# A gated convolution and token MLP on one core: the first filter block in two parts, the last copy-out on ScalarE alone, and a new order of issue

## The chip, the core and the metric

The kernel runs on one core of a Trainium2 chip. A core has a matrix engine (TensorE, PE), a vector engine (VectorE, DVE), a scalar engine (ScalarE, ACT), a general engine (GpSimd, POOL), and a sync engine (SP) that here only issues transfers. Each engine works through its own list of instructions in order, and waits at an instruction until the semaphores it names are reached. SBUF is the on-chip memory, PSUM the small memory that PE writes. The metric is the device time of one execution in microseconds (us); lower is better.

## The reference, cut to what matters

```python
# S = 2048 positions, D = 640 channels, F = 1536, all inputs bf16; x = A_q
g  = sigmoid((x * gate_w).sum(-1, keepdims=True))
# a: a short shift convolution of k, times v, then a causal convolution of length S per channel
kv = (sum of 4 shifted copies of k, weighted by shift_k) * v
y  = irfft(rfft(pad(kv)) * rfft(pad(ssm_k)))[:S]          # "filter" ssm_k is (D, S)
a  = x * (y + kv * ssm_D)
# b: an MLP over the positions
h  = layernorm(x)
u  = gelu(einsum("sd,sf->df", h, w1) + b1)
b  = (einsum("df,fs->ds", u, w2) + b2).transpose(0, 2, 1)
out = g * a + (1 - g) * b
```

## The kernel before, in words

**The MLP.** x comes in as 16 tiles of 128 positions (`xs`). DVE takes mean and variance of a tile (two `bn_stats` at L884, one `bn_aggr` at L886), POOL turns the variance into 1/sqrt (`vpe`, then `rstd`, L666 and L659), and DVE writes the normalised tile `h` (L667). PE multiplies all 16 tiles by 12 column blocks of w1 (384 matmuls, "h,w"), ACT applies gelu and writes `gT`. The second product (384 matmuls, "gT,w") has 16 groups of 24; ACT adds the bias and multiplies by 1-g on the way out (`o`).

**The convolution.** S is cut into 4 blocks of 512. A filter block i is loaded to `wnat{i}`, folded by DVE into `en` (even and odd part, L659), turned by PE (40 small matmuls against the identity, for blocks 0 and 1; blocks 2 and 3 are turned by a transposing transfer), copied from PSUM by ACT to `eo`, multiplied by cosine and sine tables `TFc` and `TFs`, which ACT makes at the start, and copied by ACT to its spectrum `W{i}`. A block of kv goes the like way: k through the shift matmuls (`kT,dg`), ACT to `ks`, a transposing transfer to `kn`, times v on DVE, DVE sums `es` and `fs`, PE by the tables `AFs` and `AFc`, ACT to the spectrum `A{j}`. DVE then multiplies spectra, 10 pairs of blocks, into `Z` (with `tT` for the second product); PE transforms each of 4 sums back ("Z,TI", 32 matmuls each), and the two halves of a result are copied out of PSUM as `pb` and `qb`, combined by DVE to `cg`, multiplied by the gated x (`xe`, scaled on ACT), and added to the output: by accumulating transfers from POOL, except the last block's forward rows, where DVE adds `o` itself and SP stores `cg`.

**What sets the order.** Every operation is declared by helpers that record it (`pe`, `act`, `tt`, `ts`, `vop`, `dma`), with its reads and writes. Nothing is emitted then. At the end `plan.run(ORDER)` emits all operations in the order of a tuple of operation numbers, numbered as they were declared. So ORDER is the order of every engine's list, of SP's and POOL's transfers too. A tracker adds the waits. PSUM is four slots (`pp0` to `pp3`), handed out in the order of emission: an operation that opens a slot gets the one that was given back first, and waits for the last reader of that slot.

The lines that the steps below touch: `W_PARTS` (how a filter block is cut for load, fold and turn), `wnat_load`, `w_turn`, and `epilogue` for the last block (`last`), where DVE makes `pb` from PSUM (L1224) while ACT makes `qb` (L701). Transfers of filter and x are at L278, `kT` at L265, POOL's gathers at L271 and its accumulating scatters at L269 and L273.

```python
W_PARTS = [((0, 2), (2, DC)) if i == 0 else ((0, DC),) for i in range(P)]   # DC = 5 chunks of 128 channels
```

The block whose turn comes first is block 1: its load is SP's first transfer, its fold is DVE's first work on data, and its turn is PE's first work. Before, it is one load, two folds and four turns of five chunks; block 0, which follows, is already cut into chunks 0-1 and 2-4.

Of the kernel before, what the change touches and what calls it, by code (L numbers as in the profile page):

```python
# [11 lines left out]
ACT = mybir.ActivationFunctionType  # L12
# [306 lines left out]
def bass_gated_mix__ssm_conv_h3__mixer_token_mlp__prompt_kernel(  # L319
# [7 lines left out]


ORDER = (
# [32 lines left out]
)  # L362


# [123 lines left out]
def _build(nc, A_q, A_k, A_v, A_shift_k, A_ssm_k, A_ssm_D, B_x, B_w1, B_b1, B_w2, B_b2, gate_w, out):  # L488
# [4 lines left out]
    P = 4  # L493
# [5 lines left out]
    DC = D // 128  # L499
# [4 lines left out]
    with ExitStack() as es:  # L504
# [237 lines left out]
        def two(p_):  # L742
            return lambda: pp[p_.slot][:, :].rearrange("p (c f) -> p c f", c=2)[:, :, 0:HD]

        def flat(p_):
            return lambda: pp[p_.slot][:, 0:D]

        def h2(ap):
            return ap.rearrange("p (c f) -> p c f", c=2)
# [112 lines left out]
        def w1t(s_, t):  # L862
            return b[f"w1_{(2 * s_ + t // 8) % 3}"][:, t % 8, :]

        W_PARTS = [((0, 2), (2, DC)) if i == 0 else ((0, DC),) for i in range(P)]

        def wnat_load(i, pr):
            for c0, c1 in W_PARTS[i]:
# [6 lines left out]
        for gi, g in enumerate(groups):  # L875
# [4 lines left out]
            for k, t in enumerate(g):  # L880
                for c in range(2):
                    o_ = b["stats"][:, t, c * 6:(c + 1) * 6]
                    i_ = xs[:, k, c * HD:(c + 1) * HD]
                    vop("DVE", 0.41, (lambda o_, i_: lambda e: e.bn_stats(o_, i_))(o_, i_), [i_], [o_], pr)  # L884
                o_, i_ = b["mv"][:, t, :], b["stats"][:, t, :]
# [28 lines left out]
        p_ = _PS()  # L914
# [9 lines left out]
        def w_turn(i):  # L924
            wn = b[f"wnat{i}"]
            en = b[f"en{i % 2}"]
            eo = b[f"eo{i % 2}"]
            for c0, c1 in W_PARTS[i]:
                fw = wn[:, c0:c1, 256:512].rearrange("p c (k u) -> p k c u", k=2)
                bw = bass.AP(tensor=wn, offset=256 + c0 * n, ap=[[DC * n, 128], [-128, 2], [n, c1 - c0], [-1, 128]])  # L930
                for e, op in ((0, ALU.add), (1, ALU.subtract)):
                    tt(en[:, 2 * e:2 * e + 2, c0 * 128:c1 * 128].rearrange("p k (c u) -> p k c u", c=c1 - c0), fw, bw, op,
                       1.0 + 0.1 * i)
            x0 = en[:, 2, :].rearrange("p (c u) -> p c u", c=DC)[:, :, 0:1]
            if i == 0:
                tt(x0, wn[:, :, 0:1], b["bf"][:, FT + NT:FT + NT + DC].rearrange("p (c o) -> p c o", o=1), ALU.add, 1.0)
            else:
                copy(x0, wn[:, :, 0:1], 1.0 + 0.1 * i, "DVE")
            if i in WTD:
                dma(eo[:, :, :, :].rearrange("p e k (c d) -> p (e k c) d", c=DC),  # L940
                    en[:, :, :].rearrange("p k d -> p (k d)"), f"eo{i % 2}", 0.5, turn=True)
                return
            for e in range(2):
                for k in range(2):
                    p_ = _PS(True)
                    for c0, c1 in W_PARTS[i]:
                        pe([p_], [(p_, c * 128, 128, en[:, 2 * e + k, c * 128:(c + 1) * 128], ident, True, True)
                                  for c in range(c0, c1)], 1.0 + 0.1 * i)
                    act(eo[:, e, k, :], flat(p_), ACT.Copy, 0.3, ps=[p_])

        def split(dst, src, pr):
            tt(dst[:, 0:2, :], src[:, 0:2, :], src[:, 2:4, :], ALU.add, pr)
# [53 lines left out]
        for s_ in range(1, NSET):  # L1006
            w1_load(s_, 2.5 if s_ < 2 else 6.0 + 2 * s_)
            for fi in range(FSET):
                p_ = _PS(True)
# [193 lines left out]
        def epilogue(m_, res, pr):  # L1203
# [13 lines left out]
            for i in range(2):  # L1217
                P_, Q_ = res[2 * i], res[2 * i + 1]
                pb, qb = (b["pb"][:, i, :], b["qb"][:, i, :]) if m_ else (b["pb0"][:, 0, :], b["qb0"][:, 0, :])
                act(h2(qb), two(Q_), ACT.Copy, 0.4, ps=[Q_])  # L1220
                if not last:
                    act(h2(pb), two(P_), ACT.Copy, 0.4, ps=[P_])
                else:
                    vop("DVE", 0.77, (lambda o_, s_: lambda e: e.tensor_copy(o_, s_()))(h2(pb), two(P_)),  # L1224
                        [two(P_)], [pb], 0.4, ps=[P_])
                if m_ == 0 or last:
                    for k, op in ((1, ALU.subtract), (0, ALU.add)):
                        c_ = cgs[k][:, i, :]
                        tt(c_, pb, qb, op, 20)
                        if last:  # L1230
                            tt(c_, c_, xes[k][:, i, :], ALU.mult, pr)
                            if k:
                                t_ = 4 * m_ + 3 - 2 * i
                                dma(rows1(out, t_), c_, f"acc1_{i}_{m_ % 2}", 1.0, stream="POOL", accum=True, idx=back(t_), whole=whole(out))
                            else:
                                tt(c_, c_, b[f"o1_{q + i}"][:, 0, :], ALU.add, pr)
                                dma(rows1(out, 4 * m_ + 2 * i), c_, "last", 1.0)
# [47 lines left out]
        p_ = _PS()  # L1285
# [43 lines left out]
```

## Time and profile before

| | |
|---|---|
| runs shown | 191.5, 192.04, 192.24 us; median 192.04 |
| the profiled execution | 191.21 us, of which its span (first to last instruction) 189.3 |
| granted TensorE clock, mean | 0.997 |
| PE busy | 175.3 us (93%), 1636 matmuls |
| DVE busy | 176.4 us (93%), 216 instructions |
| ACT busy | 111.1 us (59%), 171 instructions |
| POOL busy | 67.6 us (36%), 84 instructions |
| moved by DMA | 38.04 MB |

The profile page lists busy time by engine, the span in 40 slices, transfers, the chain of work that ended last, and the costliest groups of instructions. The timeline lists instructions in order of time as "start, duration, engine, line, operation, out<-in, shape, count"; in brackets stands the idle time of the engine just ahead and what ended it. A row with a count above 1 is several instructions run together. The list of waits has "who <- for whom: us in total, times, longest". PEld is the loading of weights beside PE; SPq are transfers as SP issues them. Where a helper records every operation all have its line (L659 for DVE's two-input operations, L701 for ACT, L310 for PE), so tiles are named.

### The profile page before, as it was taken

What the parts mean: (1) busy time and instruction counts of PE and PEld (TensorE: products, weight loads), DVE (VectorE), ACT (ScalarE), POOL (GpSimd) and SP (SyncE); (2) the same over time, 40 slices, a digit from 0 to 9 for tenths busy, and PEclk for the clock granted to TensorE, in tenths of its full rate; (3) what the DMA queues carried; (4) which work ended last, traced back from release to release, by engine and by line L of the source; (5) the groups of instructions that cost most, each with busy time, mean ns of one, the idle gap of its engine ahead of it and who ended that gap; (6) DMA issues with size and microseconds to landing.
All of it is one profiled execution on the core that took longest, in us unless ns stands there. A gap on an engine that the chain in (4) does not pass through costs nothing.

```text
span 189.3 us, 3968 instructions
## 1 busy us (share of the span) xinstructions
PE 175.3 (93%) x1636; PEld 123.5 (65%) x1636; DVE 176.4 (93%) x216; ACT 111.1 (59%) x171; POOL 67.6 (36%) x84
## 2 busy tenths in 40 slices
PE   0699999999999998999999999999999999999780
PEld 0666677666668755777777767677777777776550
DVE  4889997984999999999999999999999999999992
ACT  5889978069997077613235278633840938551660
POOL 7216557950000004000000000090058995788481
PEclk9999999999999999999999999999999999999998
DMA  4999969799994999299883568517389798696796
GB/s 146 329 248 329 361 192 237 218 272 184 244 221 126 162 257 233 68 275 236 230 205 65 118 142 239 165 40 201 117 272 281 201 207 284 117 208 192 140 149 128
DMA packets 78078, 38.04 MB, mean 201 GB/s; under 512 B 42476, under 2 KB 77548, under 8 KB 78060
## 3 DMA queue, kind: packets, MB, share of 16 engines
q1 hardware_dynamic: 75324, 32.87, 67.6%
q0 software_dynamic: 2736, 4.92, 13.2%
q8 instruction: 13, 0.21, 0.4%
q14 instruction: 5, 0.04, 0.1%
HBM read 23.08 MB, written 4.92 MB: 148 GB/s over the span
## 4 chain that ended last, share of the span: by engine, by line
PE 57%; DVE 26%; ACT 5%; issue 4%; DMA 3%; POOL 2%; DVEq 0%; POOLq 0%; ACTq 0%
PE pp L310 57%; DVE stats L884 5%; DVE W L659 5%; DMA w<-in_B_w_dram 3%; DVE Z L659 3%; DVE h L667 3%; DVE cg L659 2%; DVE kn L659 2%; DVE tT L659 2%; DVE es L659 1%; POOL vpe L666 1%; DVE mv L886 1%; DVE fs L659 1%; DVE dg L659 1%; ACT TFs L701 1%
## 5 line engine op out<-in xcount | busy, mean ns | idle before, releaser
L310 PE MATMUL pp<-h,w 128*128 128x320 bf16 x384 | 54.7, 299 | 0.3 <-ACT grow L701 0.3
L310 PE MATMUL pp<-gT,w 128*128 128x320 bf16 x384 | 53.4, 299 | 0.1
L659 DVE TENSOR_TENSOR tT<-A,W 128x5120 bf16<-128x5120 bf16 (+2 forms) x18 | 45.4, 2524 | 3.5 <-ACT A L701 3.3
L310 PEld LDWEIGHTS pp<-h,w 128*128 128x128 bf16 x384 | 36.7, 98 | 16.2 <-issue 2.1
L310 PEld LDWEIGHTS pp<-gT,w 128*128 128x128 bf16 x384 | 37.3, 98 | 14.9 <-DMA w<-in_B_w_dram 0.4
L659 DVE TENSOR_TENSOR Z<-Z,tT 128x2560 bf16<-128x2560 bf16 (+5 forms) x29 | 46.4, 1624 | 0.2
L271 POOL DMA_INDIRECT xe<-in_A_q_dram,bidx x8 | 19.4, 2428 | 62.7 <-DVE fs L659 49.2
L701 ACT ACTIVATE A<-pp 128x640 bf16<-128x640 f32 x32 | 20.6, 708 | 10.2 <-PE pp L310 9.7
L701 ACT ACTIVATE gT<-pp,bf 128x640 bf16<-128x640 f32 x12 | 9.4, 793 | 23.9 <-PE pp L310 18.4
L701 ACT ACTIVATE o<-pp,c,omg 128x640 bf16<-128x640 f32 x16 | 13.9, 880 | 14.1 <-PE pp L310 14.0
L271 POOL DMA_INDIRECT vn<-in_A_v_dram,bidx x8 | 10.4, 1294 | 31.3 <-DVE kn L659 29.8
L310 PE MATMUL pp<-Z,TI 128*128 128x320 bf16 x128 | 18.5, 299 | 1.0 <-ACT o L701 1.0
L269 POOL DMA_INDIRECT out_dram<-cg,bidx x8 | 17.8, 2229 | 2.6 <-issue 1.8
L310 PEld LDWEIGHTS pp<-Z,TI 128*128 128x128 bf16 x128 | 12.3, 98 | 6.2 <-ACT o L701 1.3
L701 ACT ACTIVATE W<-pp 128x640 bf16<-128x640 f32 x24 | 15.4, 752 | 0.4 <-PE pp L310 0.4
L884 DVE BATCH_NORM_STATS2 stats<-xs 128x6 f32<-128x320 bf16 x32 | 13.4, 465 | 0.0
L310 PE MATMUL pp<-eo,TFc 128*128 128x320 bf16 x64 | 11.7, 300 | 0.1
L659 DVE TENSOR_TENSOR Z<-A,W 128x5120 bf16<-128x5120 bf16 x4 | 11.3, 2817 | 0.0
L310 PE MATMUL pp<-eo,TFs 128*128 128x320 bf16 x64 | 11.1, 313 | 0.0
L701 ACT ACTIVATE ks<-pp 128x1024 bf16<-128x1024 f32 (+1 forms) x12 | 10.0, 900 | 1.0 <-PE pp L310 1.0
L701 ACT ACTIVATE xe<-xe,ggr 128x640 bf16<-128x640 bf16 x8 | 6.5, 822 | 6.6 <-DMA xe<-in_A_q_dram,bidx 6.5
L310 PE MATMUL pp<-idp,en 128*128 128x128 bf16 x40 | 4.5, 290 | 6.2 <-POOL cst L677 6.2
(101 smaller groups left out, 211.0 us busy)
## 6 DMA issues: line engine op xcount, KB each, us to landing
w<-in_B_w_dram SPq DMA_DIRECT2D x8, 768.0 KB
w<-in_B_w_dram SPq DMA_DIRECT2D x10, 512.0 KB, 4.6
xs<-in_A_q_dram SPq DMA_DIRECT2D x7, 320.0 KB, 5.1
wnat<-in_A_ssm_k_dram SPq DMA_DIRECT2D x3, 640.0 KB, 4.5
out_dram<-o SPq DMA_DIRECT2D x6, 320.0 KB, 4.4
vn<-in_A_v_dram SPq DMA_DIRECT2D x4, 320.0 KB, 4.1
xe<-in_A_q_dram SPq DMA_DIRECT2D x4, 320.0 KB
w<-in_B_w_dram SPq DMA_DIRECT2D x4, 256.0 KB, 5.8
```

The lines of the kernel that those rows point to most:

```text
L269: ins = engobj.indirect_dma_start(whole, off, in_ap, None, compute_op=ALU.add)
L271: ins = engobj.indirect_dma_start(out_ap, None, whole, off)
L310: ins = self.nc.tensor.matmul(ps_ap, lhsT=lhsT, rhs=rhs, start=start, stop=stop)
L659: return vop(eng, c, lambda e: e.tensor_tensor(out_, in0, in1, op), [in0, in1], [out_], pr)
L666: return e.tensor_scalar(out_, in0, s1, None, op0=op0)
L667: return e.tensor_scalar(out_, in0, s1, s2, op0=op0, op1=op1)
L701: return e.activation(out_, src, func, **kw)
L884: vop("DVE", 0.41, (lambda o_, i_: lambda e: e.bn_stats(o_, i_))(o_, i_), [i_], [o_], pr)
L886: vop("DVE", 0.16, (lambda o_, i_: lambda e: e.bn_aggr(o_, i_))(o_, i_), [i_], [o_], pr)
```

## The change

Three edits, the third of which reaches every engine.

1. `W_PARTS` cuts block 1 as block 0 is cut. Its load becomes two transfers (256 and 384 KB), its two folds four (512 and 768 elements a row), each of its four turns two steps of 2 and 3 matmuls. The sum of the work is the same; seven operations are added (719 become 726).
2. In the last block's epilogue both `pb` copies go from DVE (`tensor_copy`) to ACT.
3. ORDER is another permutation throughout.

```diff
-        W_PARTS = [((0, 2), (2, DC)) if i == 0 else ((0, DC),) for i in range(P)]
+        W_PARTS = [((0, 2), (2, DC)), ((0, 2), (2, DC)), ((0, DC),), ((0, DC),)]
...
-                    act(eo[:, e, k, :], flat(p_), ACT.Copy, 0.3, ps=[p_])
+                    if (i, e, k) in ():
+                        vop("DVE", 0.83, (lambda o_, s_: lambda q_: q_.tensor_copy(o_, s_()))(eo[:, e, k, :], flat(p_)),
+                            [flat(p_)], [eo[:, e, k, :]], 0.3, ps=[p_])
+                    else:
+                        act(eo[:, e, k, :], flat(p_), ACT.Copy, 0.3, ps=[p_])
...
-                if not last:
-                    act(h2(pb), two(P_), ACT.Copy, 0.4, ps=[P_])
-                else:
-                    vop("DVE", 0.77, (lambda o_, s_: lambda e: e.tensor_copy(o_, s_()))(h2(pb), two(P_)),
-                        [two(P_)], [pb], 0.4, ps=[P_])
+                act(h2(pb), two(P_), ACT.Copy, 0.4, ps=[P_])
```

The condition `in ()` never holds, so that piece changes nothing. Of ORDER, its ends (the middle is left out):

```diff
-    12, 11, 13, 9, 14, 10, 21, 0, 15, 22, 24, 1, 5, 23, 17, 31, 2, 155, 16, 32, 36, 26, 27, 25, 29, 28, 203, 204, 6,
...
-    717, 697, 707, 543, 708, 718, 709,
+    12, 9, 13, 11, 14, 10, 21, 22, 155, 26, 15, 5, 0, 24, 23, 27, 1, 203, 28, 204, 16, 25, 31, 217, 32, 156, 205,
...
+    720, 713, 701, 704, 663, 712, 722, 714, 721, 550, 706, 715, 716, 723, 724, 725,
```

In words, by engine and place ("i0" and "i1" are the two 128-row halves of the last block's result; c is the cosine, s the sine side):

| place | before | after |
|---|---|---|
| SP, first issues | block 1; bias row; block 0 chunks 2-4, 0-1; three bias rows; x tiles 0, 4-5; shift weights; x 1, 2-3, 6-7; k block 0 (turning); x 8-9, 14-15 ... | block 1 chunks 0-1, 2-4; bias row; block 0 chunks 2-4, 0-1; bias row; shift weights; bias row; x tile 1; bias row; x 0, 2-3, 4-5, 6-7, 10-11, 8-9; k block 0 (turning); x 14-15 ... |
| DVE, head | table indices; fold block 1 (2); indices; fold block 0; statistics | table indices; fold block 1 chunks 0-1 (2); chunks 2-4 (2); indices; fold block 0; statistics |
| PE, head | block 1: four turns; part of block 0; first table product is block 1 by TFs | one part-turn of block 1; its other seven; part of block 0; first table product is block 1 by TFc |
| ACT, head | TFs, index, TFc, TFs, index, then four `eo` | TFs, two indices, TFc, TFc, then four `eo` |
| POOL, normalisation | `vpe`/`rstd` of tile 1 before tile 0; a gather of v after both | `vpe` of tiles 0 and 1, `rstd` of 0; a gather of v; `vpe`/`rstd` of 2-3, of 4-5; then `rstd` of tile 1 |
| DVE, before the kv block 0 sums | fold of block 3 before the last `h`; `kn`, two `es`, two `fs`, fold of block 2 | fold of block 3 among the last `h`; `kn`, `es`, fold of block 2, `es`, two `fs` |
| PE, kv block 0 | w1 group, `fs` by AFs (2), w1 group, `es` by AFs (2), then AFc | `es` by AFs (2), w1 group, `fs` by AFs (2), w1 group, then AFc |
| PE, last inverse | i0 with Z of frequency rows 1, 2, 3, 0; i1 with 1, 2, 3, 0 | i0 with 1, 2, 3; i1 with 1; i0 with 0; i1 with 2, 3, 0 |
| PE, mlp groups ahead of it (a, b: first and second of a pair) | 7b, 7a, 6b; 6a is PE's last work | 7a, 7b, 6b; 6a is PE's last work |
| DVE, last Z pieces | rows 1-3 of the real half are closed after row 0's first product and its sum | rows 1-3 of the real half are closed after row 0's first product, ahead of its sum |
| ACT, end | qb i0; xe1 i1; qb i1; xe0 i1; xe0 i0; last `o` | qb i0; pb i0; pb i1; qb i1; xe1 i1; xe0 i0; last `o`; xe0 i1 |
| DVE, end | pb i0; cg1 i0 (2); pb i1; cg1 i1 (2); cg0 i0, i1; cg0 i1 (times x, plus o); cg0 i0 (times x, plus o) | cg1 i0 (2); cg1 i1 (2); cg0 i0, i1; cg0 i0 (times x, plus o); cg0 i1 (times x, plus o) |

60 rows, old and new, of the table ORDER are left out of this document.

## The prediction

> **What bounds the kernel now.** I read the page's shares first, then the list of waits of DVE, then the timeline of the head and of the tail. From the page:
>
> ```profile
> PE 175.3 (93%) x1636; PEld 123.5 (65%) x1636; DVE 176.4 (93%) x216; ACT 111.1 (59%) x171; POOL 67.6 (36%) x84
> PE 57%; DVE 26%; ACT 5%; issue 4%; DMA 3%; POOL 2%; DVEq 0%; POOLq 0%; ACTq 0%
> ```
>
> Two engines are equally full, and the chain that ended last changes between them. All of DVE's waits, from the list of waits:
>
> ```profile
> DVE tT L659 <- ACT A L701: 3.3, 1, 3.3
> DVE ncol L674 <- POOL ncol_i L767: 1.6, 1, 1.6
> DVE en L659 <- DMA wnat<-in_A_ssm_k_dram: 1.2, 1, 1.2
> DVE h L667 <- POOL rstd L659: 1.2, 1, 1.2
> DVE en L659 <- ACT bf L701: 0.6, 1, 0.6
> ```
>
> The 3.3 is the last of them in time: it ends at 45.42, with the first product into `tT`. From there to its last sum at 185.69 DVE shows no wait. So **what DVE gains before 45.4 comes out at the end, if the tail lets it**. PE has no wait over 0.1 us between 74.5 and the last inverse either. The head, from the timeline:
>
> ```profile
> 5.29 0.84 DVE L659 TENSOR_TENSOR en<-wnat 128x1280 bf16<-128x1280 bf16 x1 [1.24 <-DMA wnat<-in_A_ssm_k_dram]
> 6.19 2.53 PE L310 MATMUL pp<-idp,en 128*128 128x128 bf16 x22 [6.19 <-POOL cst L677]
> 6.94 2.49 ACT L701 ACTIVATE eo<-pp 128x640 bf16<-128x640 f32 x4 [0.47 <-PE pp L310]
> 8.51 1.27 PE L310 MATMUL pp<-eo,TFs 128*128 128x320 bf16 x4
> 11.67 0.72 PE L310 MATMUL pp<-eo,TFs 128*128 128x320 bf16 x4
> ```
>
> PE starts 0.06 us after the first fold; the "POOL cst" named as its releaser was long done. ACT waits only 0.47 for the turns. The tail:
>
> ```profile
> 175.29 0.89 ACT L701 ACTIVATE o<-pp,c,omg 128x640 bf16<-128x640 f32 x1 [2.65 <-PE pp L310]
> 176.23 4.51 PE L310 MATMUL pp<-Z,TI 128*128 128x320 bf16 x32 [0.97 <-ACT o L701]
> 176.85 0.89 DVE L659 TENSOR_TENSOR Z<-Z,tT 128x640 bf16<-128x640 bf16 x2
> 179.25 0.82 DVE L1224 CAST pb<-pp 128x640 bf16<-128x640 f32 x1
> 180.57 3.42 PE L310 MATMUL pp<-gT,w 128*128 128x320 bf16 x24
> 181.04 0.82 DVE L1224 CAST pb<-pp 128x640 bf16<-128x640 f32 x1
> 184.03 0.88 ACT L701 ACTIVATE o<-pp,c,omg 128x640 bf16<-128x640 f32 x1
> 185.20 0.49 DVE L659 TENSOR_TENSOR cg<-cg,o 128x640 bf16<-128x640 bf16 x1
> ```
>
> Z's last piece ends at 176.85 + 0.89 = 177.74, DVE's last sum at 185.69, 7.95 later; the span ends 3.6 after that (store and closing).
>
> **The change, step by step.**
>
> *1. Block 1 in parts, DVE.* Until 5.29 DVE has nothing but indices, done at 4.06. The first 256 KB of block 1 now land alone. No row shows that landing; it lies between 3.5 (the shortest landing of an x tile, 3.5 us from issue, would give 0.73 + 3.5 = 4.2) and 5.26. I take 4.2, as that transfer (160 KB) is the nearest row. Two folds of 512 elements (0.42 each, as block 0's) then lie in the old wait: 0.85. Against it, block 0's pairs of part-folds took 0.90 and whole folds 0.84 each, so cutting costs 0.12. DVE is **0.73 ahead**; with the landing at 5.26 it would be 0.12 behind. The second load is issued some 0.5 later than the one whole load; its bytes are the same, so I let it land at 5.3.
>
> *2. ACT and PE in the head.* ACT's five table operations end at 6.47 in both orders (a constant on POOL comes two small instructions later: up to 0.3), so of its 0.47 wait 0.2 to 0.47 goes. PE's first part-turn comes at about 4.8, but it then stands for the second folds and for block 0's. Up to 10.7 its matmuls run at half speed: the 4 by TFs took 1.27 at 8.51 and 0.72 at 11.67. Counted at these rates it has done three 320-wide matmuls more and three small ones fewer by then, 0.25; with ACT's gain, 24 copies of 0.62 to 0.75 in a row, I take **0.3 for PE** (ends 0 and 0.6).
>
> *3. DVE through the statistics.* The 0.62 wait for `bf` stays nearly whole (bf's matmul now stands behind two table products; I reckon 0.5). The 1.16 wait for `rstd` goes: of POOL's pairs (0.45 + 0.74) the late one now precedes its `h` by 1.7 us, by summing POOL's rows. One 0.1 operation moves ahead. Together 0.73 + 0.1 + 1.16 - 0.1 = 1.9 earlier at the product `kn`: 33.8 in place of 35.7, 34.6 by summing the new order's rows piece by piece. `kn` itself is ready at about 30.7 (before, its last transposing transfer was issued at 27.3; they take 3.4).
>
> *4. The way to the first Z.* Fold of block 2 (1.75) now precedes the second `es`, where before it filled the 3.3 wait. From `kn` the `fs` end after 1.41 + 5 x 0.8 + 1.6 = 40.5 to 41.1; before, 40.36. So the 1.3 of step 3 is spent here, to shrink the wait; PE does the `es` products first (1.1), which were after. Then the four AFs copies need one matmul pair and ACT (0.6 + 3 x 0.7, a gelu among them): `tT` starts at 43.5 to 43.8 (45.42). The product by A's cosine side needs four more copies behind a w1 group and a gelu: 46.9 to 47.3 against 48.25 before. DVE **gains 1.3** here; I bound it by 0.7 (ACT alone 0.75 ahead) and 1.7.
>
> *5. The middle.* PE's small waits at 40.05 (0.44), 71.2 (0.53) and 73.5 to 74.5 (0.34) stood before `fs` and `es` products; the new order puts a gate product and the sine side first, so I count them gone: with 0.3, PE is up to 1.6 ahead. DVE's list is nearly the old one; comparing sums of rows, `kn` of block 1 comes after its transfers, the W sums after their copies by 0 to 1. What a wait here would cost is bounded by 0 and 3.3, the longest that DVE shows; I take 0.
>
> *6. The tail.* The 0.97 before the inverse goes: counted through ORDER, its first slots are given back by older groups. But Z bounds it: rows 1-3 close one operation (0.82) earlier, at 176.08 - 0.82 - 1.3 = 174.0, and row 0 at 177.74 - 1.3 = 176.45, one step (0.55) later needed. Thence: four steps 2.2, last mlp group 3.4, `o` 0.9, then `xe0 i1`, now behind `o`, 0.75, and two operations of DVE 1.0: 8.3 after Z. Before it was 7.95. The casts (2 x 0.82) leave DVE, but DVE then waits for `o`, so this buys nothing; ACT's two copies (0.70 each) lie in the time when it waits for the last group. The end therefore moves by **-1.3 + 0.35 = -0.95**. If the inverse could start with PE alone (173.7), Z would still hold it.
>
> *Queues moved past.* The k transfer, which holds SP from 6.89 to 12.05, is now issued after x tiles 8 to 11, about 8.0; its product is needed at 20. The w1 and w2 loads keep their places up to one.
>
> **The sum.** 191.21 (the profiled execution; 189.3 and 1.9 around) - 0.95 = 190.3; the median stands 0.83 above that execution: 192.04 - 1.0 = **191.0**.
>
> **The rivals.**
>
> *A. The gain dies on the way* (chance 0.22). Only 0.4 of DVE's lead reaches Z, because ACT's copies hold it: they run without pause from 44.1 to past 60. For it: ACT is 9/10 busy there. Against: ACT also starts earlier. Then -0.4 + 0.35: 192.0.
>
> *B. Slow clock* (0.08). The half speed lasted 4.5 us from PE's first matmul, and PE was never idle in them. If it is unbroken work that ends it, the new order's stands only from about 7.8 on, after its waits for folds, and half speed lasts to 12.3: 1.6 us of it lose 0.8, and the `fs` products and `tT` come 0.4 to 0.8 later. Then -1.3 + 0.7 + 0.35: 191.8. Against: one execution can't say what ended it. [...]
>
> *C. Slower: POOL's chain* (0.18). `rstd` of tile 1 now stands behind a gather and two pairs, and PE's second w1 step needs its `h`; tile 8's pair stands behind another gather. The slack of either is 1.7 to 1.9 by POOL's rows with gathers at 1.29 (v's mean). A gather at 2.43 (x's mean) adds 1.14, two 2.3. From 1.8 on each us is lost by DVE; at 3.6 all of 1.3 and 0.5 more: 0.35 + 0.6 slower, 193.0. For it: this wait was there before, 1.16. Against: v's gathers are the same ones.
>
> *D. More than forecast* (0.08): step 3's lead passes whole (1.9), and DVE's saved casts shorten the tail: 190.1.
>
> The forecast has 0.44, from 190.5 to 191.6. **Range** 190.1 to 193.0, the ends of C and D.
>
> 0.5% (0.96 us) is about what a measurement here can tell. The forecast lies on that bound: six tenths of it and D are faster, 0.34; A, B and the rest of the forecast the same, 0.48; C slower, 0.18.
>
> **What would show it.** Step 1: first fold before 5.0, and a row of 512 elements ahead of PE's start. 3: no `h <- rstd` wait in DVE's list. 4: `tT` before 44.2, the next `Z` before 47.4. 5: DVE without waits from there. 6: no 0.97 ahead of the inverse, Z's last piece at 176.4, the last sum 8.3 later, and DVE waiting for ACT in between. Wrong if a wait of over 0.5 stands in DVE's list after 47, or the first fold starts after 5.2.

## The result, and the profile after

The changed kernel took 190.32 us (median of 7 runs, 189.77 to 191.4), the kernel before 192.09 beside it (7 runs); the ratio is 0.9919, 95% interval 0.9895 to 0.9942. The forecast was 191.0, range 190.1 to 193.0. Measured a second time, 12 runs beside 35 of before, the changed kernel took 191.36 against 191.85: 0.9977 (0.9959 to 0.9996). Both intervals lie below 1, and they do not overlap; by how much the kernel is faster is the question of most of what follows.

The profiled execution of the changed kernel took 190.03 us, its span 188.0 (before: 191.21 and 189.3). From its page, the busy shares and the chain that ended last:

```profile
PE 175.3 (93%) x1636; PEld 124.1 (66%) x1636; DVE 175.2 (93%) x216; ACT 112.6 (60%) x173; POOL 65.1 (35%) x84
...
PE 89%; DMA 7%; DVE 1%; ACT 0%; ACTq 0%; SPq 0%; issue 0%
```

PE and DVE are as full as before. That the chain now names PE alone means only that the walk back from the end took PE's side of two parallel full engines. The list of waits says more (DVE <- whom: us in total, times, longest):

```profile
DVE tT L659 <- ACT A L701: 2.6, 1, 2.6
...
DVE cg L659 <- ACT pb L701: 1.0, 1, 1.0
DVE en L659 <- DMA wnat<-in_A_ssm_k_dram: 0.9, 2, 0.7
DVE en L659 <- ACT bf L701: 0.7, 1, 0.7
...
DVE Z L659 <- ACT A L701: 0.5, 1, 0.5
```

The wait of `h` for `rstd` (1.2 before) is gone, the one for `A` is 0.7 shorter, and a new one for the copy `pb` stands in the tail. The head, from the timelines of DVE and of PE:

```profile
3.84 0.77 DVE L659 TENSOR_TENSOR en<-wnat 128x512 bf16<-128x512 bf16 x2 [0.21 <-DMA wnat<-in_A_ssm_k_dram]
...
5.58 1.04 DVE L659 TENSOR_TENSOR en<-wnat 128x768 bf16<-128x768 bf16 x2 [0.69 <-DMA wnat<-in_A_ssm_k_dram]
...
43.76 2.83 DVE L659 TENSOR_TENSOR tT<-A,W 128x5120 bf16<-128x5120 bf16 x1 [2.63 <-ACT A L701]
47.12 2.83 DVE L659 TENSOR_TENSOR Z<-A,W 128x5120 bf16<-128x5120 bf16 x1 [0.54 <-ACT A L701]
```

```profile
4.67 0.61 PE L310 MATMUL pp<-idp,en 128*128 128x128 bf16 x4 [4.67 <-DVE par_i L666]
6.20 2.87 PE L310 MATMUL pp<-idp,en 128*128 128x128 bf16 x23 [0.93 <-DVE en L659]
```

The first part is folded 1.45 earlier than block 1 was (5.29), PE starts at 4.67 and stands again to 6.20, and `tT` starts at 43.76 in place of 45.42. The tail:

```profile
171.45 3.43 PE L310 MATMUL pp<-gT,w 128*128 128x320 bf16 x24 [1.57 <-DMA w<-in_B_w_dram]
...
174.72 4.51 PE L310 MATMUL pp<-Z,TI 128*128 128x320 bf16 x32
...
175.44 0.90 DVE L659 TENSOR_TENSOR Z<-Z,tT 128x640 bf16<-128x640 bf16 x2
...
182.22 1.55 POOL L269 DMA_INDIRECT out_dram<-cg,bidx  x1 [0.30 <-DVE cg L659]
182.53 0.89 ACT L701 ACTIVATE o<-pp,c,omg 128x640 bf16<-128x640 f32 x1 [0.53 <-PE pp L310]
...
184.69 0.49 DVE L659 TENSOR_TENSOR cg<-cg,o 128x640 bf16<-128x640 bf16 x1
```

The last piece of Z ends at 176.34 (177.74 before), DVE's last sum at 185.18 (185.69), the span at 188.0. So 1.40 of lead reach Z, 0.51 the last sum, and 1.3 the end: between last sum and end 0.8 came from somewhere that the prediction had taken as fixed. By its own signs the prediction was already in trouble here: it called itself wrong if a wait of over 0.5 stood in DVE's list after 47, and one of 0.54 stands at 47.12.

Six moments of every trace, in us from the start of its span, carry most of what follows. "bf" is the start of the small operation `en<-wnat,bf` of block 0, the one that waits for `bf`; "second tT" is the product into `tT` with kv block 1.

| kernel | bf | kn | first tT | second tT | last Z ends | span |
|---|---|---|---|---|---|---|
| before | 12.11 | 35.67 | 45.42 | 76.31 | 177.74 | 189.3 |
| changed | 12.46 | 34.85 | 43.76 | 74.98 | 176.34 | 188.0 |
| changed, again (e5) | 12.12 | 34.52 | 43.43 | 75.93 | 177.29 | 189.3 |
| e1 new head, old rest | 12.72 | 35.12 | 44.69 | 76.20 | 177.64 | 189.6 |
| e2 old head, new rest | 11.93 | 35.49 | 45.24 | 76.40 | 177.76 | 189.5 |
| e3 changed, block 1 whole | 12.14 | 34.53 | 43.44 | 75.92 | 177.28 | 189.4 |
| e9 changed, gate product late | 12.08 | 34.47 | 43.38 | 74.61 | 176.90 | 188.7 |
| e10 before, `rstd` moved | 12.52 | 36.64 | 46.39 | 77.28 | 178.72 | 190.8 |
| e11 block 1 whole, gate late | 12.37 | 34.76 | 43.68 | 74.91 | 176.38 | 188.4 |
| e12 before, block 1 in parts | 11.76 | 35.31 | 45.06 | 75.95 | 177.40 | 189.5 |

Read across, the columns keep fixed distances. In the new order the first `tT` comes 31.30 after "bf" and 8.91 after `kn`, within 0.02, in all of these but e1; in the old order 33.31 and 9.75 (e10, whose edit lies between, aside from the first). From the second `tT` to the last Z it is 101.4 in all but e9. DVE sets the pace, and these moments are where it can be set back.

### The profile page after: what moved, and what is told of

The parts are those of the page before. It is cut to its first block, busy times and chain, and to the rows that moved or that the text cites. A ratio compares the mean times of both kernels' runs of the same rounds, so it can differ in the third digit from the quotient of the medians.

```text
span 188.0 us, 3972 instructions
## 1 busy us (share of the span) xinstructions
PE 175.3 (93%) x1636; PEld 124.1 (66%) x1636; DVE 175.2 (93%) x216; ACT 112.6 (60%) x173; POOL 65.1 (35%) x84
## 4 chain that ended last, share of the span: by engine, by line
PE 89%; DMA 7%; DVE 1%; ACT 0%; ACTq 0%; SPq 0%; issue 0%
PE pp L310 89%; DMA w<-in_B_w_dram 4%; DMA wnat<-in_A_ssm_k_dram 2%; DVE cg L659 1%; ACT o L701 0%; ACTq L322 0%; DVE en L659 0%; SPq L278 0%
## 5 line engine op out<-in xcount | busy, mean ns | idle before, releaser
L271 POOL DMA_INDIRECT xe<-in_A_q_dram,bidx x8 | 20.6, 2575 | 66.3 <-PE pp L310 48.7
L271 POOL DMA_INDIRECT vn<-in_A_v_dram,bidx x8 | 9.4, 1170 | 32.5 <-DVE kn L659 31.4
L269 POOL DMA_INDIRECT out_dram<-cg,bidx x8 | 15.5, 1936 | 2.9 <-issue 1.8
L310 PE MATMUL pp<-eo,TFc 128*128 128x320 bf16 x64 | 12.6, 321 | 0.0
L310 PE MATMUL pp<-eo,TFs 128*128 128x320 bf16 x64 | 10.5, 300 | 0.0
L310 PE MATMUL pp<-kT,dg 64*64 64x256 bf16 x320 | 9.8, 270 | 0.0
```

The lines of the kernel that those rows point to most:

```text
L269: ins = engobj.indirect_dma_start(whole, off, in_ap, None, compute_op=ALU.add)
L271: ins = engobj.indirect_dma_start(out_ap, None, whole, off)
L310: ins = self.nc.tensor.matmul(ps_ap, lhsT=lhsT, rhs=rhs, start=start, stop=stop)
```

## The experiments

Each was timed in five rounds beside the kernel before; the ratio is to that kernel, with its 95% interval.

### Head or rest: e1 and e2

The order was cut at the first product into `Z` (eleven of the operations lie on different sides of that point in the two orders), and the two heads and rests were crossed.

```diff
 e1: ORDER = changed kernel's up to the first Z product + what is left, in the order of before; pb copies on DVE
 e2: ORDER = before's up to the first Z product + what is left, in the changed order; block 1 whole; pb copies on ACT
```

> The changed kernel's order up to the first product into Z, block 1 in parts; from there the order of the kernel before, with the pb copies on DVE. Theory (the gain is DVE's lead at about 44 us, handed through a DVE without waits): tT starts at 43.8, the last Z piece ends about 1.3 earlier than before's 177.74, the end 1.3 earlier than before's: 190.8 us. Rival (the gain is made in the tail, by the casts off DVE and the last scatter): the lead is lost on the way, 191.7 to 192.1. Second rival (the head's lead dies in ACT's copies after 44): last Z piece at 177.3 or later.

> The reverse: block 1 whole and the order of the kernel before up to the first product into Z; from there the changed kernel's order, with the pb copies on ACT. Theory: last Z piece at 177.7 as before; last DVE sum 8.8 after it in place of 8.0, but the closing 0.8 shorter, so 192.0 plus or minus 0.4. Rival (gain made in the tail): 190.3 to 191.0, with the last scatter of POOL issued over 0.8 earlier after the last Z piece than before.

Measured: e1 191.01 beside 191.78, 0.9958 (0.9930 to 0.9987). e2 191.92, 0.9996 (0.9974 to 1.0019). By the times the gain goes with the head: e1 is faster than before, e2 is not told apart from it, though the two intervals overlap a little. That the rest of the order and the copies bring nothing by themselves holds within e2's interval, some -0.5 to 0.4 us; its trace also has a wait of 0.66 at 76 us. The traced execution of e1 is one of its slowest (191.89; the 12 runs lie between 189.6 and 192.1) and doesn't show the gain: `tT` stands at 44.69, not 43.8, where DVE waited 3.3 for `A` in place of 2.6; PE had stayed at half speed to 14.2 (below), which is the likely cause; the next Z is 0.11 earlier than before, and so is all that follows.

### The parts: e3 and e12

```diff
-        W_PARTS = [((0, 2), (2, DC)), ((0, 2), (2, DC)), ((0, DC),), ((0, DC),)]
+        W_PARTS = [((0, 2), (2, DC)) if i == 0 else ((0, DC),) for i in range(P)]
```

e3 is the changed kernel with this line and its order otherwise kept; e12 is the kernel before with the opposite edit, each pair of parts side by side in its old place.

> The changed kernel with block 1 in one load, two folds, four turns, its order otherwise the same. Theory: the first fold starts at 5.3 in place of 3.84, DVE is 0.7 later at the first waits and tT 0.4 to 0.8 later; 190.7 to 191.1. If the parts are worth nothing (the waits for bf and ACT's A copies take all of it): tT at 43.8 still and 190.3. If the order leans on the parts (PE's first matmul at 6.2, slow clock until 12 or later, turns late for ACT): 191.5 or more.

> The kernel before with block 1 in two parts (load, folds, turns, each pair of parts side by side in its old place) and nothing else; pb copies on DVE as before. Theory from the runs so far (the parts bring nothing, what DVE gains is spent in its wait for bf, and PE's broken start may keep it at half speed longer): first fold at 3.6 to 4.1, kn at 35.5 to 36.2, tT 9.75 later, 191.6 to 192.4 beside about 191.8 of before. Steps 1 and 2 of the prediction (DVE 0.73 ahead, PE 0.3): kn at 34.8 to 35.2, 191.0 to 191.3.

Measured: e3 191.59 beside 191.78, 0.9986 (0.9964 to 1.0007); e12 191.65 beside 191.64, 0.9998 (0.9974 to 1.0022). In e3 `tT` starts at 43.44, no later than with the parts (43.76 and 43.43): what e3 lost against the first measurement it lost at 72 us, as the changed kernel's own repeat did. In e12, from the list of DVE's waits:

```profile
DVE tT L658 <- ACT A L700: 3.3, 1, 3.3
...
DVE h L666 <- POOL rstd L658: 1.2, 1, 1.2
DVE stats L883 <- DMA xs<-in_A_q_dram: 0.7, 1, 0.7
DVE en L658 <- DMA wnat<-in_A_ssm_k_dram: 0.3, 1, 0.3
```

The wait for the first block is 0.9 shorter than before and the one for `bf` is gone, but a new one of 0.7 for an x tile stands just ahead of that operation and takes most of the lead; `kn`, `tT` and the last Z are 0.34 to 0.36 earlier, and the end is not (the last scatter took 5.05 to land, 4.57 before). **The parts bring 0.0 to 0.35 on their own, and nothing in the new order.**

The new order with and without the parts shows where the lead goes. With them (e5) DVE has done all that stands ahead of the operation "bf" at 11.31, without them (e3) at 12.08; it starts at 12.12 and at 12.14, since `bf` itself ends at 12.09 and 12.10. And where `bf` was early, at 10.93 in e8, DVE waited 0.66 for an x tile and started at 11.99.

### The tail: e4, e6, e7 and e8

e4 puts both `pb` copies of the last block back on DVE. e6 shortens the way to POOL's last scatter, e7 the way to SP's last store, e8 does both. In ORDER's last numbers, 550 is the last `o`, 706 the scaling of xe0 i1, 715 and 716 are the sum of cg0 i0 with that `o` and its store, 723 to 725 the product, sum and store of cg0 i1; 696 and 697 are i0's row 0 and i1's row 1 on PE, 707 is the scaling of xe1 i1, 718 the copy `pb` i1, which e6 and e8 give to DVE:

```diff
 e4
-                act(h2(pb), two(P_), ACT.Copy, 0.4, ps=[P_])
+                if not last:
+                    act(h2(pb), two(P_), ACT.Copy, 0.4, ps=[P_])
+                else:
+                    vop("DVE", 0.77, (lambda o_, s_: lambda e: e.tensor_copy(o_, s_()))(h2(pb), two(P_)),
+                        [two(P_)], [pb], 0.4, ps=[P_])
 e7
-    720, 713, 701, 704, 663, 712, 722, 714, 721, 550, 706, 715, 716, 723, 724, 725,
+    720, 713, 701, 704, 663, 712, 722, 714, 721, 706, 550, 723, 724, 725, 715, 716,
 e6
-    691, 694, 695, 661, 660, 697, 696, 708, 662, 698, 699, 709, 710, 700, 718, 549, 711, 717, 553, 707, 719, 720,
+    691, 694, 695, 661, 660, 696, 697, 708, 662, 698, 699, 709, 707, 710, 700, 549, 711, 718, 717, 553, 719, 720,
```

> The changed kernel with the last block's two pb copies back on DVE, at the same places of the order; nothing else changed. Theory on record (casts off DVE buy nothing, DVE waits for o anyway): 190.3, the last DVE sum at 185.2 to 185.5. Rival (the copies stood ahead of the last scatter, and the closing hangs on POOL, whose drain ends 5.6 to 5.7 after that scatter is issued): scatter issued 0.5 to 1.0 later than 182.22, end 0.5 to 1.0 later, 190.8 to 191.3.

> The changed kernel with the chain to POOL's last scatter shortened: PE does i0's row 0 ahead of i1's row 1, ACT scales xe1 i1 right after pb i0, and pb i1 is copied by DVE. Theory (the end is the later of two: 1.3 us after the last scatter lands, or the last SP store's landing plus 0.4): scatter issued about 0.5 earlier after the last Z piece than in the changed kernel (5.4 in place of 5.9), but the last SP store unchanged, so the end moves by 0 to -0.2. If only the scatter counts: -0.5. If only the last DVE sum counts: 0.

> The changed kernel with the chain to the last SP store shortened: ACT scales xe0 i1 ahead of the last o, DVE finishes cg0 i1 (whose o is old) and SP stores it before cg0 i0 waits for the last o. The last DVE sum ends about 1.1 earlier (7.7 after the last Z piece in place of 8.84). Theory (the end hangs on the last scatter, 1.3 us after its landing): end unchanged, within 0.1. The prediction's own step 6 (the end follows the last DVE sum): 1.1 earlier.

> Both edits together. Theory: 0.4 to 0.6 earlier than the changed kernel, the last scatter still the last to land. If only the last DVE sum counts: 1.1. If neither chain sets the end: 0.

Measured: e4 191.57 beside 191.78, 0.9985 (0.9963 to 1.0008). e6 191.05, e7 191.15, e8 191.36, all beside 191.85: 0.9973 (0.9943 to 1.0003), 0.9957 (0.9934 to 0.9980), 0.9984 (0.9956 to 1.0012). Against the repeat of the changed kernel, 191.36, none is told apart by its time. The traces tell more: the landing of a transfer, the end of POOL's closing drain and the end of the span stand in their records.

| kernel | last Z ends | last DVE sum ends | last scatter issued | it lands | span ends | from landing to end |
|---|---|---|---|---|---|---|
| before | 177.74 | 185.69 | 183.36 | 187.93 | 189.32 | 1.39 |
| changed | 176.34 | 185.18 | 182.22 | 186.63 | 188.02 | 1.39 |
| changed, again | 177.29 | 185.65 | 182.73 | 187.93 | 189.31 | 1.39 |
| e4 `pb` on DVE | 178.07 | 186.42 | 184.28 | 188.74 | 190.13 | 1.39 |
| e6 scatter chain | 177.43 | 186.33 | 182.87 | 187.52 | 188.91 | 1.39 |
| e7 store chain | 177.78 | 185.53 | 183.21 | 188.31 | 189.70 | 1.39 |
| e8 both | 177.11 | 184.90 | 182.55 | 187.74 | 189.13 | 1.39 |

**The span ends 1.39 after the last scatter has landed, in all 14 traces**; POOL's drain ends 1.16 after that landing. From DVE's last sum to the end it is anything from 2.58 (e6) to 4.23 (e8), while from the last Z to the end it is 11.58 before, 11.68 in the changed kernel and 11.48 to 12.13 in the others: the new tail neither gains nor loses anything that these traces can tell. e7 brought the last sum 0.6 nearer to Z (7.75 after it, 8.36 in the repeat), and from Z to the end it took 11.92 (12.02). From its timeline, POOL's issues and DVE's last sums:

```profile
181.28 1.63 POOL L269 DMA_INDIRECT out_dram<-cg,bidx  x1 [0.30 <-DVE cg L658]
183.21 1.84 POOL L269 DMA_INDIRECT out_dram<-cg,bidx  x1 [0.30 <-issue]
```

```profile
184.63 0.89 DVE L658 TENSOR_TENSOR cg<-cg,o 128x640 bf16<-128x640 bf16 x2
```

The second scatter is issued 2.3 before the last sum ends at 185.53, and the end is 1.39 after it lands at 188.31, though SP's last store lands at 188.72. The edit of e6 did not shorten its chain: the scatter is issued 5.44 after Z, exactly as in the repeat, because PE there waits 0.65 for Z's row 0 anyway; its shorter end (11.48) is a faster landing (4.65 in place of 5.20), and that varies from trace to trace between 4.41 and 5.30. e4 had one flaw: `pb` of i1 stood ahead of i0's product on DVE, so the scatter was issued 6.21 after Z; it landed 10.67 after Z all the same (10.64 in the repeat). That landing follows POOL's queue, whose transfers land one after another (in the changed kernel's trace at 183.68, 184.88 and 186.63); that this queue sets it is argued, not shown.

### The repeat, and the gate product: e5, e9 and e11

e1 to e4 differ from the changed kernel in the head or the tail, yet three of them waited 0.7 to 1.4 at 76 us, where its first trace shows 0.1. So the kernel itself was run again.

> The changed kernel once more, beside the kernel before on one chip, because two variants that differ from it in the head or the tail alone showed a wait of 1.4 us at 75 us (a product of a gate whose end reached the other engines 2.2 us late) that its own trace does not have. If that stop is met by chance in some executions of any order: the changed kernel's times spread from 189.6 to 191.6 with a median of 190.3 to 191.0. If it is absent from this order: 189.8 to 190.6 with nothing above 191. If the edits of the two variants cost what their medians said: 190.3 and no late end in the trace.

Measured: 191.36 beside 191.85, 0.9977 (0.9959 to 0.9996). The spans of its 12 runs are 189.0 to 190.1; of the first 7 runs, six had 187.9 to 188.5. Its timeline at the place, PE and ACT:

```profile
69.51 0.46 PE L310 MATMUL pp<-xT,gwc 128*32 128x128 bf16 x20
...
69.91 0.72 PE L310 MATMUL pp<-es,AFs 128*128 128x320 bf16 x4
...
70.46 0.71 PE L310 MATMUL pp<-es,AFc 128*128 128x320 bf16 x4
...
72.15 0.28 ACT L700 ACTIVATE grow<-pp 128x128 f32<-128x128 f32 x1 [2.30 <-PE pp L310]
...
72.48 0.72 PE L310 MATMUL pp<-es,AFc 128*128 128x320 bf16 x4 [1.32 <-ACT grow L700]
```

and the same place in the first trace of the changed kernel:

```profile
69.84 0.46 PE L310 MATMUL pp<-xT,gwc 128*32 128x128 bf16 x20
70.24 0.72 PE L310 MATMUL pp<-es,AFs 128*128 128x320 bf16 x4
70.79 1.25 PE L310 MATMUL pp<-es,AFc 128*128 128x320 bf16 x8
```

```profile
70.36 0.28 ACT L701 ACTIVATE grow<-pp 128x128 f32<-128x128 f32 x1 [0.18 <-PE pp L310]
```

The matmuls are recorded at the same pace in both. But in the repeat the signal that the gate product (`xT,gwc`) is done reaches the others at 72.13, 2.16 after its recorded end, and the signals of the next two products come within 0.12 of it. ACT stands at `grow`, the `A` copies stand behind it, PE's next product stands for the PSUM slot that `grow` gives back, and DVE's second `tT` comes 1.38 late. The ends of PE's records are modelled, as the profile's own legend says, so they can't say what stood.

The late signal is in the trace of before too, 1.25, but there two of the four table products stand ahead of the gate product, and DVE's list shows no wait for it. So the next edit moves the gate product:

```diff
-    431, 414, 415, 591, 306, 565, 432, 379, 425, 380, 390, 381, 391, 383, 384, 385, 388, 389, 382, 392, 393, 592, 396,
-    593, 418, 397, 596,
+    431, 591, 306, 565, 432, 379, 425, 380, 390, 381, 391, 383, 384, 385, 388, 389, 382, 392, 393, 592, 396, 414, 593,
+    418, 397, 415, 596,
```

(414 is the gate product, 415 its copy `grow`; the numbers between are table products, `A` copies and DVE's sums.)

> The changed kernel with the first gate product moved on PE from ahead of the four table products of kv block 1 that DVE waits for to behind them, and its copy on ACT likewise. In the repeats of the changed kernel's order the end of that product reached the other engines 2.16 us late, and DVE waited 1.38 for ACT's copies. Theory (the late end belongs to that product or to its stretch of DMA, and its place in the new order lets it stop ACT and so DVE): the wait at 76 falls to 0.3 or less, the last Z piece ends 1.1 to 1.4 earlier than in the repeat (177.29), 190.0 to 190.4. Rival (the stop comes at that time whatever PE does): the wait stays, 191.3.

> The changed kernel with block 1 whole again (PE starts at 6.2 without a break) and the gate product late. Theory (the parts bring nothing; a broken start of PE leaves it at half speed for 7.0 to 9.3 us in place of 4.4, which costs tT 0 to 1.2): as the run with the gate product alone or up to 0.5 better, 189.8 to 190.4; half speed ends near 10.7. If the parts bring DVE's lead as the prediction has it: 0.5 to 0.8 slower than the run with the gate product alone.

Measured, both beside 191.74: e9 190.69, 0.9944 (0.9922 to 0.9967); e11 190.20 (6 runs), 0.9915 (0.9887 to 0.9943). In both the gate product's own signal is on time, and the second `tT` starts with a wait of 0.10, at 74.61 and 74.91. The row of e5, then that of e11:

```profile
75.93 2.82 DVE L658 TENSOR_TENSOR tT<-A,W 128x5120 bf16<-128x5120 bf16 x1 [1.38 <-ACT A L700]
```

```profile
74.91 2.83 DVE L658 TENSOR_TENSOR tT<-A,W 128x5120 bf16<-128x5120 bf16 x1
```

The table products at that time still signal their end up to 0.6 (e9) and 0.8 (e11) late, so some of the stop stays, as the rival had it; what the edit takes away is its way to ACT's copies and DVE. e11 and e3 differ by the gate product's place alone: 190.20 and 191.59, and their intervals lie apart. e11, the old block 1 in the new order with the gate product late, also lies below the interval of the changed kernel's repeat (0.9959 to 0.9996); e9's interval overlaps it, so that the gain of e9 over the repeat is not shown by the times. e9's trace has another wait of 0.84 for `A` copies at 115.7; a w1 load came 1.2 late for PE at 80, but that this made the wait is not shown:

```profile
81.24 2.35 PE L310 MATMUL pp<-h,w 128*128 128x320 bf16 x16 [1.23 <-DMA w<-in_B_w_dram]
```

### A lead at kn: e10

The kernel before with only the pair of POOL's that DVE waited for moved ahead:

```diff
-    143, 118, 119, 134, 135, 144, 115, 275, 276, 46, 141, 114, 145, 251, 152, 284, 252, 123, 124, 125, 126,
+    143, 118, 119, 123, 124, 134, 135, 144, 115, 275, 276, 46, 141, 114, 145, 251, 152, 284, 252, 125, 126,
```

> The kernel before with one pair of POOL's small operations (the rstd that DVE waited 1.16 for at 33.2) moved ahead of two other pairs, nothing else. Theory (step 3: a lead of DVE ahead of kn passes through fs and A to tT, and from there to the end): kn 0.9 to 1.2 earlier than 35.67, tT 0.6 to 1.1 earlier than 45.42, 191.0 to 191.3 beside 191.85. Rival (ACT's copies of A set tT whatever DVE does): tT at 45.2 to 45.5 and no change.

Measured: 192.75 beside 191.74, 1.0049 (1.0027 to 1.0072): slower. From its timeline, POOL's pair and DVE's folds beside it:

```profile
30.43 0.37 POOL L665 TENSOR_SCALAR vpe<-mv 128x2 f32<-128x2 f32 x1 [3.62 <-DVE mv L885]
30.89 2.33 POOL L658 TENSOR_TENSOR rstd<-vpe,cst 128x2 f32<-128x2 f32 x1
...
34.62 0.77 POOL L658 TENSOR_TENSOR rstd<-vpe,cst 128x2 f32<-128x2 f32 x1
```

```profile
31.07 1.58 DVE L658 TENSOR_TENSOR en<-wnat 128x1280 bf16<-128x1280 bf16 x2
33.33 0.80 DVE L666 TENSOR_SCALAR h<-xs,mv,rstd 128x640 bf16<-128x640 bf16 x2 [0.68 <-POOL rstd L658]
```

The statistics were not there before 30.43, so the pair could not start earlier; its `rstd` took 2.33 while DVE folded, 0.77 alone; and the two pairs behind it became late as well: the wait for `rstd` is 1.5 in three pieces. As a cure it failed. As a measurement of what passes it is the cleanest run here: `kn` 0.97 later, `tT` 0.97, the last Z 0.98, DVE's last sum 0.99, the median 1.0. (Of the 0.97, 0.41 stood already at "bf", ahead of the edit; the rest is the longer wait and some 0.2 of smaller steps.)

The kernel before shows the like at the same place, POOL's pair beside the fold of block 3:

```profile
30.52 1.97 POOL L666 TENSOR_SCALAR vpe<-mv 128x2 f32<-128x2 f32 x2 [0.47 <-DVE mv L886]
```

```profile
30.67 1.57 DVE L659 TENSOR_TENSOR en<-wnat 128x1280 bf16<-128x1280 bf16 x2
```

The first of these two `vpe` took 1.80, where one without a fold beside it took 0.22. The changed order has that fold later, among the last `h` (at 32.81 and 34.10), when POOL's pairs are done, and there none of them took over 1.01. So the move of the fold may be worth as much as the move of the pair; no run has the fold's move alone, and none shows why an operation of POOL takes longer beside a fold.

## Why the prediction was right, and where it was not

The forecast of -1.0 lies between the two measurements, -1.8 and -0.5. Its chain of steps holds in the middle and fails at both ends. That the sum came out near is in part luck: the lead of steps 1 and 2 did not come, step 4 made up for it, and the later last sum did not count, because it does not set the end. In the repeat the wait that step 5 took as 0 cost 1.38.

*Step 1 (parts, DVE 0.73 ahead) failed.* The landing was even earlier than taken (first fold at 3.84, taken 4.2). But the lead ended at the wait for `bf`, which the prediction named and took as 0.5: it was 0.68, and the operation behind it started at 12.46, 0.35 later than before. A lead ahead of a wait for another engine is that wait's to take: e5 reached this place 0.77 ahead of e3 and left it 0.02 ahead. Taking the parts out (e3) left `tT` where it was; putting them into the kernel before (e12) moved `kn` by 0.36 and the end by nothing.

*Step 2 (PE gains 0.3) failed.* By 10.7 PE was to have begun three 320-wide matmuls more and three small ones fewer; it had begun one more (two in e5) and three fewer, which is worth nothing. And its broken start left it longer at half speed (a 320-wide matmul starts every 0.27 us there, every 0.14 later, in both kernels): the last matmul that took as long as at half speed (0.31 for 128 columns, 0.45 or more for 320; 0.22 and 0.30 at full speed) stands at 11.74, at 10.43 before. That is what rival B foresaw, near its size (12.3). From the first matmul to the last at half speed it is 4.2 to 5.0 in the five traces with an unbroken start (before, e2, e3, e10, e11). With a pause of 0.5 to 1.4 in the first 4 us it is 6.1 to 9.2 in seven (7.07 in the changed kernel, 6.99 in its repeat, 9.2 in e1), but 4.4 in e8 and 4.9 in e12. So a pause alone doesn't decide it, and what ends the half speed is not shown; the granted clock is recorded as 1.00 from 4 to 12 us in both kernels. What it costs is not what rival B priced: most of it only lengthens the wait for `bf` (that operation started at 12.9 at the latest, in e4), and only in e1 did `tT` come later than its distance from "bf", by 0.66.

*Step 3 (the 1.16 wait for `rstd` goes) held.* From "bf" to `kn` it is 22.39, before 23.56: 1.17 less. That the pair's earlier place alone did it is not shown, as the fold of block 3 moved too (e10). `kn` came at 34.85, not 33.8 to 34.6, by the loss of steps 1 and 2. *Rival C* did not occur, but e10 shows that its price, one for one, was right.

*Step 4 held.* `tT` was foreseen at 43.5 to 43.8 and came at 43.76; the next Z at 46.9 to 47.3, and 47.12. From `kn` to `tT` it is 8.91 in place of 9.75. So the 1.66 at `tT` are 1.17 + 0.84 less 0.35. *Rival A* took a part: the next Z waits 0.54 for copies of `A`, which it did not before, and 1.33 of the 1.66 are there at the second `tT`. From there on nothing is lost: Z's last piece is 1.40 earlier.

*Step 5 (the middle costs nothing)* is the step that decides between the two measurements. The prediction counted the new order's gate product ahead of the copies as a gain for PE; it bounded a wait there by 0 and 3.3 and took 0. In the first trace that wait was 0.10, in the repeat 1.38.

*Step 6 had the right Z and the wrong end.* Z's last piece was foreseen at 176.45 and ended at 176.34. To the last sum it took 8.84, not 8.3 (8.36 in the repeat, as foreseen): PE had waited 1.57 for the last w2 load (8.0 from issue to landing, 6.55 before), so row 0 was transformed 0.55 later than Z allowed, and `xe0 i1` stood behind `o` as foreseen. But the term that failed is the one that was not worked out at all: "the span ends 3.6 after that (store and closing)". The end follows the last scatter's landing. That scatter was issued 1.14 earlier than before (182.22, 183.36: the 1.40 at Z less 0.26) and landed 0.16 faster, and this, not the last sum, is why 1.3 of the lead came out in that trace. *Rival D* said the saved copies would shorten the tail; e4 gives no sign of it, with the flaw named above.

What stays open: what holds the gate product's signal. It was late by 2.1 to 2.2 in the six other traces of the new order with the product at its new place (e3 to e8), and not in the first one. But the stop is not that product's alone: the gate product is 1.0 to 1.7 late in before, e1, e2 and e10, the table products up to 0.8 in e9 and e11, and only the first trace of the changed kernel and e12 have none. Nothing in the records of PE, DMA or POOL at that time differs in a way that was tested. The chip is a rival that was not tested either: e1 to e4 ran on one, e5 to e8 on a second, e9 to e11 on a third, e12 on a fourth, and that of the first measurement is not on record, so that e11 and e3 are compared only through the kernel before beside each. Nor is it known in how many executions of the first measurement the stop was absent; their spans suggest six of seven.

## What to carry to other kernels

Before counting a lead, find the next place where the leading engine waits for another: a gain ahead of it (the parts, 0.73 foreseen) is gone there, while of one behind it (1.66 at `tT`) 1.40 reached the end of DVE's full stretch, and a loss of 0.97 (e10) passed whole. Follow the end of the span backward from what lands last, with the closing of each engine, before pricing the last arithmetic: here 14 traces end 1.39 after one POOL transfer, wherever DVE's last sum is. And in a list that an engine works through in order, a small product that others don't need yet is best put behind the copies that they do need, since its signal can come late (here 2.2) for a reason that the trace does not show; one trace doesn't tell that, a repeat does.

## What the runs showed of the hardware

- A product's completion signal came 2.16 after its recorded end, and the next two products' signals within 0.12 behind it, while the matmuls themselves were recorded at their usual pace (e5; 2.12 to 2.17 in e3, e4, e6, e7 and e8 as well).
- PE's half-speed stretch at the start (a 320-wide matmul every 0.27, every 0.14 later, with the granted clock recorded as 1.00, in before and in the changed kernel) lasted 4.2 to 5.0 in the five traces with an unbroken start and 4.4 to 9.2 in the nine with a broken one.
- One of POOL's operations on 128x2 elements took 2.33 beside DVE's two-input folds, 0.77 without (e10); another 1.80, 0.22 without (before).
- The span ended 1.39 after POOL's last accumulating scatter landed, and 1.16 of that was POOL's drain.
